# The transpose of one batch's q moved from TensorE to a DMA, in a fused attention and feed-forward kernel

## The chip, the cores and the metric

The kernel runs on one core of one Trainium2 chip. The metric is the device time of one execution in microseconds (us); medians are given with their extremes where a small difference matters. Every run quoted here is of the fast state, the undisturbed one. Ratios are computed as the mean time of one kernel's fast runs over the mean of the other kernel's fast runs in the same rounds, so they are not quite the ratio of the medians quoted beside them.

## The reference

Attention with keys and values averaged over groups of eight positions, then a feed-forward layer with the activation h cos(h):

```python
# q, k, v: (8 batches, 8 heads, 576 positions, 64) float32
k_p = k.reshape(B, H, Sp, 8, D).mean(axis=3)          # Sp = 72
v_p = v.reshape(B, H, Sp, 8, D).mean(axis=3)
attn = softmax(q @ k_p.T / sqrt(D))                   # per batch and head
x = (attn @ v_p), heads side by side                  # 4608 tokens x 512
h = x @ w_in                                          # 512 -> 2048
out = (h * cos(h)) @ w_out                            # 2048 -> 512
```

## The kernel before

Scores are computed as k_pooled (stationary) times q transposed, so q of each batch is transposed in bf16 from 128 partitions x 2304 to 18 blocks of 128x128. For batches 2 to 7 a DMA issued from the SP queue does this from SBUF to SBUF. For batches 0 and 1 TensorE does it, into PSUM, from where VectorE and ScalarE copy it:

```python
    def q_transpose(b):                                   # by DMA
        qT_tile(b)
        nc.sync.dma_start_transpose(out=att["qT", b], in_=q_flat(b))

    def q_transpose_mm(b, bank, g0, g1):                  # on TensorE
        ...
        for g in range(g0, g1):
            nc.tensor.matmul(ps[:, g - g0, :], q_flat(b)[:, g * 128:(g + 1) * 128], identity, is_transpose=True)
        return lambda copy: copy(out=att["qT", b][:, g0:g1, :], in_=ps)
```

Behind the loads for batch 0, the next loads go out in this order, all from GpSimd, converted from float32 to bf16 on the way:

```python
    for cg in range(3):
        load_w_in(cg)
    load_even(staged["k", 1], 1, k)
    load_even(staged["q", 1], 1, q, 0, 2)      # first half of q of batch 1
    load_w_in(3)
    load_even(staged["q", 1], 1, q, 2, 4)      # second half
    load_w_out(0)
    load_even(staged["v", 1], 1, v)
    ...
    for cg in range(1, 4):
        load_w_out(cg)
```

The tile loop has an up phase (x times w_in, eight groups `fp` of eight matmuls) and a down phase (times w_out). Batch b = t + 1 has its attention interleaved in the down phase of tile t. Only for t = 0 are pooled k and transposed q made on TensorE, between the up groups:

```python
            up_mm(t, fp, 2 if fp < 2 else 0)
            between = ()
            if t == 0:
                if fp == 4:
                    puts = pool_k_mm(1, obanks[0], 0, 2), pool_k_mm(1, obanks[1], 2, 4)
                elif fp in (5, 6):
                    g0 = 9 * (fp - 5)
                    puts = q_transpose_mm(1, obanks[0], g0, g0 + 5), q_transpose_mm(1, obanks[1], g0 + 5, g0 + 9)
                if fp in (4, 5, 6):
                    puts[0](vec)
                    between = ((puts[1], act),)
            up_g(t, fp, between)
        ...
        if t == 0:    # (after so many down matmuls, do this)
            fill[1:] = [(2, S_(0, 0)), (8, lambda: pool_v_mm(1, banks[1])), ..., (18, S_(2, 2)), ...]
        ...
        if 0 < t and b + 1 < B:      # later loads wait until k of this batch has been transposed
            nc.gpsimd.tensor_copy(out=gate, in_=kk[b % 2][0:1, 0, 0:1])
```

`S_(0, 0)` is the first scores unit of batch 1.

The softmax here doesn't subtract the row's maximum and nothing guards it: scores larger than these inputs give would overflow.

Of the kernel before, what the change touches and what calls it, by code (L numbers as in the profile page):

```python
# [19 lines left out]
def kernel(  # L20
# [52 lines left out]
    obanks = [psum.tile([128, 512], FP32, name=f"obank{i}") for i in range(2)]  # L73
# [33 lines left out]
    def load_q(b):  # L107
        q_tile(b)
        load_even(staged["q", b], b, q)
# [6 lines left out]
    def load_w_out(cg):  # L116
        nc.gpsimd.dma_start(
            out=w_out_sb[cg],
            in_=moe_w_out[cg * 512:(cg + 1) * 512, :].rearrange("(f p) m -> p f m", p=128))
# [30 lines left out]
    def pool_k_mm(b, bank, pj0, pj1):  # L150

        kb = staged["k", b]
        ps = bank[:, 0:(pj1 - pj0) * Sp].rearrange("p (j n) -> p j n", n=Sp)
        for pj in range(pj0, pj1):
            for t in range(ROW):
                for rows in half:
                    nc.tensor.matmul(ps[rows, pj - pj0, :], lhsT=kb[rows, pj, t, :], rhs=groups[rows, t, :],  # L157
                                     start=(t == 0), stop=(t == ROW - 1))
        return lambda copy: put_kk(b, ps, pj0, pj1, copy)
# [10 lines left out]
    def k_transpose(b):  # L170
        nc.sync.dma_start_transpose(out=kk[b % 2], in_=kp2[b % 2].rearrange("p h s d -> p (h s d)"))
# [4 lines left out]
    def qT_tile(b):  # L176
        att["qT", b] = asb.tile([128, QB, 128], BF16, name="qT", tag="qT")

    def q_flat(b):
        return staged["q", b].rearrange("p j t d -> p (j t d)")  # L180

    def q_transpose(b):
        qT_tile(b)
        nc.sync.dma_start_transpose(out=att["qT", b], in_=q_flat(b))

    def q_transpose_mm(b, bank, g0, g1):

        if ("qT", b) not in att:
            qT_tile(b)
        ps = bank.bitcast(BF16)[:, 0:(g1 - g0) * 128].rearrange("p (g n) -> p g n", n=128)  # L190
# [3 lines that stand above are left out]
# [6 lines left out]
    def scores(b, u, pair):  # L200
        scores_mm(b, u, pair)
        scores_exp(b, u, pair)
# [32 lines left out]
    def values(b, u, pair, later=None):  # L235

        (c0, n), (h0, nh) = u
        ex = att.pop(("ex", b, u))
        for i in range(nh):
            pj, hp = divmod(h0 + i, 2)  # L240
            nc.tensor.matmul(pair[:, hp, (i // 2) * n:(i // 2 + 1) * n],  # L241
                             lhsT=vz[b % 2][:, pj, 2 * hp:2 * hp + 2, :].rearrange("p a d -> p (a d)"),
                             rhs=ex[:, ex_col(u, i):ex_col(u, i) + n])
        w = nh * n // 2
        lnc, inv = inverse_tile(w)
        for hp in range(2):
            nc.scalar.activation(out=lnc[half[1 - hp]], in_=pair[half[1 - hp], hp, 0:w], func=ACTF.Ln)  # L247
        nc.scalar.activation(out=inv, in_=lnc, func=ACTF.Exp, scale=-1.0)  # L248

        def mul():  # L250
            for hp in range(2):
                nc.vector.tensor_mul(out=x_out(b, u, half[hp]), in0=cols(pair[half[hp], hp, :], u),  # L252
                                     in1=cols(inv[half[1 - hp]], u))

        if later is None:
            mul()
        else:
            later.append(mul)
# [25 lines left out]
    def exp_tables():  # L284
        nc.scalar.preload_act_table_set("natural_log_exp_and_others")  # L285

    def sin_tables():
        nc.scalar.preload_act_table_set("trig_and_small")  # L288


    def up_mm(t, fp, k0=0, k1=KCH):

        h = banks[fp % 3]
        for j in range(2):
            fc = 2 * fp + j
            for ki in range(k0, k1):
                nc.tensor.matmul(h[:, j, :], lhsT=w_in_sb[fc // 4][:, ki, (fc % 4) * 128:(fc % 4 + 1) * 128],  # L297
                                 rhs=xT[:, ki, t * TILE:(t + 1) * TILE],
                                 start=(ki == 0), stop=(ki == KCH - 1))

    def up_g(t, fp, between=()):
        h = banks[fp % 3]
        cos = msb.tile([128, 2, TILE], FP32, name="cos", tag="cos", bufs=2)
        nc.scalar.activation(out=cos, in_=h, func=ACTF.Sin, bias=half_pi[:, :1])  # L304
        for put, copy in between:
            put(copy)
        nc.vector.tensor_mul(out=g_sb[:, 2 * fp:2 * fp + 2, :], in0=h, in1=cos)  # L307
# [78 lines left out]
    for cg in range(1, 4):  # L386
        load_w_out(cg)

    def warm_up(n, bank):

        for i in range(n):
            nc.tensor.matmul(bank, lhsT=warm[:, 0:128], rhs=warm)
# [7 lines left out]
    puts = q_transpose_mm(0, banks[2][:, 0, :], 0, 5), q_transpose_mm(0, obanks[0], 5, 9)  # L400
# [24 lines left out]
    for t in range(NT):  # L425
        b = t + 1
        if t > 0:

            up_mm(t, 0, 0, 2)
            up_mm(t, 1, 0, 2)  # L430
        for fp in range(FFCH // 2):
            up_mm(t, fp, 2 if fp < 2 else 0)
            between = ()
            if t == 0:
                if fp == 4:
                    puts = pool_k_mm(1, obanks[0], 0, 2), pool_k_mm(1, obanks[1], 2, 4)
                elif fp in (5, 6):
                    g0 = 9 * (fp - 5)
                    puts = q_transpose_mm(1, obanks[0], g0, g0 + 5), q_transpose_mm(1, obanks[1], g0 + 5, g0 + 9)
                if fp in (4, 5, 6):  # L440
                    puts[0](vec)
                    between = ((puts[1], act),)
            up_g(t, fp, between)
            if 0 < t and b < B:
                if fp == 0:
                    q_transpose(b)
                elif fp == 2:
                    k_transpose(b)
        mms = [(ms, fc) for ms in range(4) for fc in range(FFCH)]
        if t == 0:  # L450
            mms = [(ms, fc) for hm in range(2) for cg in range(4) for ms in range(2 * hm, 2 * hm + 2)
                   for fc in range(4 * cg, 4 * cg + 4)]


        def S_(n, bank):
            return lambda: scores(b, us[n], banks[bank])

        later = []

        def V_(n, bank, wait=None):  # L460
            return lambda: values(b, us[n], banks[bank], wait)

        fill = []
        if t < B:
            exp_tables()
            fill = [(1, lambda: scores(t, REST, banks[2])), (16, lambda: values(t, REST, banks[1]))]
        if t == 0:
            fill[1:] = [(2, S_(0, 0)), (8, lambda: pool_v_mm(1, banks[1])), (8, lambda: values(t, REST, banks[2])),
                        (11, S_(1, 0)), (13, V_(0, 1)), (18, S_(2, 2)), (21, V_(1, 0, later)), (26, S_(3, 1)),
                        (32, lambda: later.pop()()), (32, V_(2, 2)), (40, V_(3, 0))]  # L470
        elif b < B:
            us = BY_TOKENS

            def scores_of(*parts):

                def go():
                    for f in scores_mm, scores_exp:
                        for b_, u, bank in parts:
                            f(b_, u, banks[bank])
                return go  # L480

            fill = [(4, scores_of((b, us[0], 2), (b, us[1], 0))), (14, V_(0, 1, later)), (16, lambda: later.pop()()),
                    (19, V_(1, 2)), (35, scores_of((b, us[2], 0), (b, us[3], 1), (t, REST, 2))),
                    (38, V_(2, 0)), (43, lambda: values(t, REST, banks[1])), (46, V_(3, 2))]
        fi = 0
        if t == NT - 1:
            mms = mms[:-FFCH]
        for n, (ms, fc) in enumerate(mms):
            while fi < len(fill) and fill[fi][0] <= n:
                fill[fi][1]()  # L490
                fi += 1
            down_mm(obanks[ms % 2], ms, fc)
            if fc == FFCH - 1:
                down_out(t, ms, obanks[ms % 2])
        if t < B:
            sin_tables()
        if 0 < t and b + 1 < B:

            nc.gpsimd.tensor_copy(out=gate, in_=kk[b % 2][0:1, 0, 0:1])  # L499
        if b + 1 < B:  # L500
            load_kv(b + 1, "k", k)
            load_q(b + 1)
            load_kv(b + 1, "v", v)
            pool_add(b + 1, "k")
            pool_add(b + 1, "v")
# [29 lines left out]
```

## Time and profile before

| | before |
|---|---|
| median (lowest, highest) | 302.22 us (302.09 to 302.62) |
| span of the profiled execution | 301.4 us |
| TensorE busy | 97% |
| DMA engines busy, 8 to 48 us | 1.2 on the scale where 1 is one packet in flight per engine |
| transposed q of batch 1 first read at | 35.51 us |

The profile lists per engine when instructions ran and what ended the idleness ahead of them. L192 is the line of the TensorE transposes, L297 the up matmuls, L310 the down matmuls, L211 the scores. PEld is TensorE's weight load, which overlaps its matmuls; SPq and POOLq are queues from which DMAs are issued; q0 is the DMA queue of the loads that GpSimd issues, q1 that of what SP issues. The profiled execution of the kernel before took 303.21 us, 1.0 us more than the median.

### The profile page before, as it was taken

The numbers are of one execution on the slowest core, as the hardware profiler recorded it, in microseconds if no ns is written. First come the engines' busy times: TensorE is split into PE (matmuls) and PEld (weight loads), VectorE is DVE, ScalarE is ACT, GpSimd is POOL, SyncE is SP. The second block draws the span as 40 slices with busy tenths as digits, with TensorE's granted clock in tenths as the row PEclk, the third lists the DMA queues.
The fourth block names the chain that finished last, engine by engine and source line by source line (L and its number), as shares of the span: only waits on it lengthen the run. The fifth ranks groups of instructions, "written<-read, shape, count | busy, mean of one in ns | idle before, by whom it ended". The sixth has DMA issues, their size and how long they took to land.

```text
span 301.4 us, 4625 instructions
## 1 busy us (share of the span) xinstructions
PE 293.9 (97%) x1816; PEld 143.2 (48%) x1816; DVE 170.8 (57%) x212; ACT 205.7 (68%) x254; POOL 130.4 (43%) x93
## 2 busy tenths in 40 slices
PE   8789999999999999999999999999999999999995
PEld 3445544445544454445444544455444544444444
DVE  5448637465467446754666556654775477425712
ACT  3786798469876987688778886789668966605500
POOL 8463016984983398239913990389300000000000
PEclk9999999999999999999999999999999999999999
DMA  7999999639526961697079617791811130131023
GB/s 152 197 207 206 206 205 195 141 55 176 117 60 124 167 127 29 146 158 140 6 170 143 129 36 171 94 174 39 141 32 35 37 70 0 37 70 35 0 67 75
DMA packets 44165, 32.91 MB, mean 109 GB/s; under 512 B 22128, under 2 KB 39408, under 8 KB 44144
## 3 DMA queue, kind: packets, MB, share of 16 engines
q0 software_dynamic: 19744, 18.07, 38.3%
q1 hardware_dynamic: 24160, 14.42, 20.5%
q8 instruction: 14, 0.23, 0.3%
q10 hardware_dynamic: 240, 0.13, 0.2%
q14 instruction: 7, 0.06, 0.1%
HBM read 36.70 MB, written 9.44 MB: 153 GB/s over the span
## 4 chain that ended last, share of the span: by engine, by line
PE 93%; DMA 4%; POOL 1%; DVE 1%; issue 0%; POOLq 0%; DVEq 0%
PE bank L297 41%; PE obank L310 41%; PE bank L241 5%; DMA kv_st<-in_v_dram 4%; PE bank L211 3%; PE bank L328 1%; PE bank L165 1%; POOL q_b L84 1%; PE obank L157 0%; PE obank L280 0%; PE obank L192 0%; DVE xT L282 0%; DVE vz L167 0%; POOL kv_st L84 0%; DVE o_sb L316 0%
## 5 line engine op out<-in xcount | busy, mean ns | idle before, releaser
L310 PE MATMUL obank<-w_out_sb,g_sb 128*128 128x512 bf16 x560 | 131.4, 379 | 0.0
L297 PE MATMUL bank<-xT,w_in_sb 128*128 128x512 bf16 x576 | 126.6, 379 | 0.0
L304 ACT ACTIVATE cos<-bank,half_pi 128x1024 f32<-128x1024 f32 x72 | 79.3, 1113 | 59.5 <-PE bank L297 59.5
L307 DVE TENSOR_TENSOR g_sb<-bank,cos 128x1024 bf16<-128x1024 f32 x72 | 87.3, 1223 | 43.0 <-ACT cos L304 42.9
L297 PEld LDWEIGHTS <-w_in_sb 128*128 128x128 bf16 x576 | 56.1, 98 | 67.6 <-issue 1.6
L310 PEld LDWEIGHTS <-g_sb 128*128 128x128 bf16 x560 | 52.8, 98 | 56.5 <-issue 2.0
L252 DVE TENSOR_TENSOR xT<-bank,inv 64x512 bf16<-64x512 f32 (+1 forms) x72 | 45.3, 629 | 40.8 <-ACT inv L248 40.1
L141 POOL TENSOR_TENSOR kv_st<-kv_st 72x2048 f32<-72x2048 bf16 x12 | 48.7, 4058 | 33.9 <-DMA kv_st<-in_k_dram 33.9
L247 ACT ACTIVATE lnc<-bank 64x512 f32<-64x512 f32 (+1 forms) x72 | 39.2, 544 | 3.1 <-PE bank L241 1.7
L316 DVE COPY o_sb<-obank 128x512 f32<-128x512 f32 x35 | 23.6, 689 | 30.9 <-PE obank L310 30.5
L218 ACT ACTIVATE ex<-bank 72x1024 bf16<-72x1024 f32 (+1 forms) x40 | 35.0, 929 | 8.5 <-PE bank L211 8.4
L142 POOL TENSOR_TENSOR kv_st<-kv_st 72x1024 f32<-72x1024 f32 x12 | 28.2, 2349 | 1.0
L248 ACT ACTIVATE inv<-lnc 128x512 f32<-128x512 f32 (+1 forms) x36 | 21.0, 583 | 1.1
L241 PE MATMUL bank<-ex,vz 72*128 72x256 bf16 (+1 forms) x176 | 20.0, 243 | 0.0
L241 PEld LDWEIGHTS <-vz 72*128 72x128 bf16 x176 | 13.6, 97 | 9.6 <-DVE xT L252 0.5
L145 POOL TENSOR_TENSOR kp<-kv_st 72x512 bf16<-72x512 f32 x12 | 14.9, 1263 | 0.5
L211 PE MATMUL bank<-qT,kk 64*72 64x256 bf16 (+1 forms) x192 | 13.2, 252 | 0.0
L211 PEld LDWEIGHTS <-kk 64*72 64x72 bf16 x192 | 7.4, 109 | 9.9 <-issue 7.2
L285 ACT ACT_TABLE_LOAD x9 | 11.5, 1283 | 0.9 <-PEq L519 0.7
L499 POOL COPY gate<-kk 1x1 bf16<-1x1 bf16 x5 | 0.9, 179 | 25.7 <-DMA kk<-kp 25.7
L288 ACT ACT_TABLE_LOAD x9 | 11.5, 1283 | 0.2
L103 POOL DMA_DIRECT2D kv_st<-in_v_dram x6 | 5.0, 841 | 8.8 <-PE bank L165 8.8
(55 smaller groups left out, 93.1 us busy)
## 6 DMA issues: line engine op xcount, KB each, us to landing
out_dram<-o_sb SPq DMA_DIRECT2D x70, 128.0 KB, 2.4
kv_st<-in_v_dram POOLq DMA_DIRECT2D x8, 576.0 KB, 13.7
kv_st<-in_k_dram POOLq DMA_DIRECT2D x7, 576.0 KB, 7.6
q_b<-in_q_dram POOLq DMA_DIRECT2D x6, 576.0 KB, 9.9
w_in_sb<-in_moe_w_in_dram POOLq DMA_DIRECT2D x4, 512.0 KB, 14.5
w_out_sb<-in_moe_w_out_dram POOLq DMA_DIRECT2D x4, 512.0 KB, 18.1
q_b<-in_q_dram POOLq DMA_DIRECT2D x4, 288.0 KB, 13.0
g_sb<-in_k_dram SPq DMA_DIRECT2D x1, 576.0 KB, 3.7
```

The lines of the kernel that those rows point to most:

```text
L141: add(out=s, in0=x[:, :, 0:4, :], in1=x[:, :, 4:8, :], op=ADD)
L142: add(out=s[:, :, 0:2, :], in0=s[:, :, 0:2, :], in1=s[:, :, 2:4, :], op=ADD)
L211: nc.tensor.matmul(pair[:Sp, bank, c:c + n].rearrange("p (g n) -> p g n", n=64), lhsT=kk[b % 2][half[r], h0 + i, 0:Sp], rhs=att["qT", b][h ...
L218: nc.scalar.activation(out=ex[:, 0:nh * n].rearrange("p (a n) -> p a n", a=2), in_=pair[:Sp, :, 0:nh * n // 2], func=ACTF.Exp, scale=scale ...
L241: nc.tensor.matmul(pair[:, hp, (i // 2) * n:(i // 2 + 1) * n], lhsT=vz[b % 2][:, pj, 2 * hp:2 * hp + 2, :].rearrange("p a d -> p (a d)"), ...
L247: nc.scalar.activation(out=lnc[half[1 - hp]], in_=pair[half[1 - hp], hp, 0:w], func=ACTF.Ln)
L252: nc.vector.tensor_mul(out=x_out(b, u, half[hp]), in0=cols(pair[half[hp], hp, :], u), in1=cols(inv[half[1 - hp]], u))
L297: nc.tensor.matmul(h[:, j, :], lhsT=w_in_sb[fc // 4][:, ki, (fc % 4) * 128:(fc % 4 + 1) * 128], rhs=xT[:, ki, t * TILE:(t + 1) * TILE], st ...
L304: nc.scalar.activation(out=cos, in_=h, func=ACTF.Sin, bias=half_pi[:, :1])
L307: nc.vector.tensor_mul(out=g_sb[:, 2 * fp:2 * fp + 2, :], in0=h, in1=cos)
L310: nc.tensor.matmul(o, lhsT=g_sb[:, fc, ms * 128:(ms + 1) * 128], rhs=w_out_sb[fc // 4][:, fc % 4, :], start=(fc == 0), stop=(fc == FFCH - 1))
L316: nc.vector.tensor_copy(out=o[:, 0:n], in_=ps)
```

## The change

The intent is to take 18 transposes and their four copies off the engines at a place where TensorE is the bound, and to let an idle DMA queue do them, as it already does for the later batches.

```diff
     for cg in range(1, 4):
         load_w_out(cg)
 
+    q_transpose(1)
+
     def warm_up(n, bank):
 ...
                 if fp == 4:
                     puts = pool_k_mm(1, obanks[0], 0, 2), pool_k_mm(1, obanks[1], 2, 4)
-                elif fp in (5, 6):
-                    g0 = 9 * (fp - 5)
-                    puts = q_transpose_mm(1, obanks[0], g0, g0 + 5), q_transpose_mm(1, obanks[1], g0 + 5, g0 + 9)
-                if fp in (4, 5, 6):
                     puts[0](vec)
                     between = ((puts[1], act),)
```

## The prediction

> **What bounds the kernel now.** I read the busy table and the chain that ended last on the page, then the timeline of 28 to 47 us, where the change acts, and then the loads by landing time.
>
> ```profile
> PE 293.9 (97%) x1816; PEld 143.2 (48%) x1816; DVE 170.8 (57%) x212; ACT 205.7 (68%) x254; POOL 130.4 (43%) x93
> ...
> PE 93%; DMA 4%; POOL 1%; DVE 1%; issue 0%; POOLq 0%; DVEq 0%
> ```
>
> TensorE is busy 97% of the span and is 93% of the chain. Its instructions run in program order, so an instruction taken off it is worth its time, and an instruction that waits moves the whole rest of the kernel back by that wait. The timeline (start, length, engine) around the two places where q of batch 1 is now transposed:
>
> ```profile
> 28.43 1.90 PE L297 MATMUL bank<-xT,w_in_sb 128*128 128x512 bf16 x8
> ...
> 30.16 0.67 PE L192 MATMUL obank<-identity,q_b 128*128 128x128 bf16 x9
> ...
> 30.66 1.89 PE L297 MATMUL bank<-xT,w_in_sb 128*128 128x512 bf16 x8
> ...
> 32.39 0.67 PE L192 MATMUL obank<-identity,q_b 128*128 128x128 bf16 x9
> ...
> 32.89 1.89 PE L297 MATMUL bank<-xT,w_in_sb 128*128 128x512 bf16 x8
> ...
> 34.62 0.38 PE L310 MATMUL obank<-w_out_sb,g_sb 128*128 128x512 bf16 x1
> ...
> 35.51 0.41 PE L211 MATMUL bank<-qT,kk 64*72 64x256 bf16 x4
> ```
>
> A group of eight up matmuls with nine transposes takes 30.66 - 28.43 = 2.23 us, a group without them 34.62 - 32.89 = 1.73 us. The last line is the first reader of the transposed q of batch 1: it follows only two down matmuls and the last scores of batch 0, 35.51 us into the span. That is the **deadline**.
>
> Meanwhile the DMA engines are full. In the table of two-microsecond stretches (the last two columns are DMA share and GB/s), every row from 8 us to 48 us looks like these two, and they fall off only after 50 us:
>
> ```profile
> 30.00:32.00 2.00, 2.00 (x18) 1.18 (x17) 1.45 (x3) 1.59 (x2) 0.00 (x0) 1.00 1.23 207
> 34.00:36.00 2.00, 2.00 (x19) 0.84 (x18) 0.99 (x2) 1.34 (x3) 0.00 (x0) 1.00 1.23 205
> ```
>
> So the loads are a backlog, one after another. The second half of q of batch 1 is issued at 11.41 us (operation on its tile, window 11 to 12 us) and lands 18.9 us later, at **30.3 us**:
>
> ```profile
> L84 POOL DMA_DIRECT2D q_b<-in_q_dram x1: 696/696/696, 11.4 to 11.4; - x1
> ...
> DMA to landing us min/median/max: 18.9/18.9/18.9
> ```
>
> By the same reckoning (issue plus time to landing) w_out 0 lands at 32.9, v of batch 1 at 35.7, w_out 1 at 38.2, w_out 2 at 40.7, w_out 3 at 43.3, k of batch 2 at 47.7, q of batch 2 at 50.0 us. Only v of batch 2 is not yet issued (38.7 us, after the pooling of v of batch 1 has freed its buffer).
>
> **What the Trainium skill says.** (1) VectorE: DVE Perf Modes, section The three transpose paths, gives 390 ns for a 128x128 bf16 transpose on TensorE and 1309 ns by DMA. The trace is better for both: nine on TensorE cost 0.50 us of its time (56 ns each), and a DMA of 18 blocks lands in 4.2 us, 0.23 us a block. (2) Advanced Engine Details and Errata, section X-Bar Transpose (TRN2), says that transposing DMAs are as fast as ordinary ones, and speaks of 16-row wavefronts. The trace agrees on the rate in a free moment (1133 packets, 290 GB/s between 59 and 60 us). (3) DMA: Bandwidth & Descriptors, section Queues, rings and completion order, says that each DMA engine goes round-robin between its queues and switches only between whole packets. The trace agrees that a sharing queue is slowed: see below. (4) TensorE: Matmul & The Clock Gate, Part 1, says that TensorE falls to half rate after some 3.4 us of idleness and needs as long of work to get back. The trace shows the cold state at its start: ten 128x512 matmuls take 4.45 us, 0.445 us each, against 1.73 / 8 = 0.216 us later.
>
> **The change part by part.**
> Removed: 18 transposes on TensorE in two groups of nine, 2 x (2.23 - 1.73) = **1.0 us** off the path; also two copies of 0.49 us on VectorE and two of 0.58 us on ScalarE, which lie beside up matmuls that are the longer (1.73 us against 1.23 + 0.49 and 1.11 + 0.58) and are worth nothing.
> Added: one DMA transpose of 128x2304 bf16 on the SP queue, which has nothing else to do before its first output at 46.05 us. It can start when the second half of q has landed: 30.3 us, plus about 0.25 us from a landing to the start of what it releases (w_in 3 lands at 28.9, the issue that waits for it starts at 29.17), so 30.55 us. The deadline is 35.51 - 1.0 = 34.5 us. That leaves 4.0 us. The six such transposes of later batches need 4.2 us from issue to landing (4.1 to 5.6) with the load queue empty. So even undisturbed it would be just late, by about half a microsecond, counting 0.25 us again for the reader.
>
> But here it isn't undisturbed. No transpose in this trace runs beside loads: the kernel holds the loads of later batches back until a transpose has landed (the one-element copy "gate"). So I size it from two other things.
> First, output writes, which share the SP queue. On the page 70 of them have a median of 2.4 us; those issued between 45.9 and 47.2 us, beside the loads, took 5.1 us, though each has only 64 packets, four per DMA engine:
>
> ```profile
> out_dram<-o_sb SPq DMA_DIRECT2D x70, 128.0 KB, 2.4
> ```
>
> ```profile
> q0 software_dynamic: 249, 0.27, 123.3%
> out_dram<-o_sb SPq DMA_DIRECT2D x2, 128.0 KB, 5.1
> ```
>
> That is 2.7 us more for four packets: 0.7 us a turn on the slowest engine (estimate).
> Second, the last transpose (214.8 us, 5.6 us to landing). In tenths of a microsecond its traffic runs at some 110 packets, then a single instruction fetch (16 KB: 0.23 MB in 14) occupies one engine, and all sixteen stop for 0.5 us and crawl until 219.4 us. A transpose moves at the pace of its slowest engine.
> The transpose has some 2304 packets of 256 bytes, 144 per engine, and takes 2.0 us of pure transfer (2304 / 1133 a us); the other 2.2 us of 4.2 are fixed. If it changes turns after 16 rows (the wavefront; my choice, no trace shows it), it has nine turns: 9 x 0.7 = 6.3 us of waiting if each turn is a slow one, 9 x 0.3 = 2.7 us if they are average ones (in 48.0 to 49.0 us 48 output packets passed on 16 engines, one per 0.33 us). So landing takes 4.2 + 2.7 = 6.9 to 4.2 + 6.3 = 10.5 us. I take **10 us**, near the slow end because of the lockstep.
> The first scores then start at 30.55 + 10 + 0.25 = 40.8 us in place of 35.51: **+5.3 us**, with the 1.0 us saved already in it. TensorE stands idle some 40.8 - 34.5 = 6.3 us, more than the 3.4 us, so it will run the next 3.4 us or so of work at half rate: about **+1.7 us**. Sum: +7.0 us, 302.2 + 7.0 = 309.2, say 309.
> Moved: the transpose takes 2 us of all DMA engines from the loads, so w_out 1 to 3 land 2 us later (40.2, 42.7, 45.3). Their first uses come at 38.6 us (w_out 1) and later before; delayed by 5 us they no longer wait. Later stages should just shift: k and q of batch 2 have 6 us to spare (the transposed k lands at 62.5 us, read at 68.8).
>
> **The rivals.**
> A: *the transfer is hidden*. It needs landing within 4 us, which not even the free ones did. And without the wait for q, w_out 1 takes its place: it landed at 38.2 for a use at 38.6 us; 1.0 us earlier and with the load 2 us later, TensorE would wait for it until 40.4. So the gain of 1.0 us cannot be had, and the least I expect is +1.5 us, 303.7. A real gain of 2% is out of reach: only 1.0 us is removed.
> B: *mild sharing*: landing in 6 to 8 us, scores 1.3 to 3.3 us late, little or no cold clock: 303.7 to 306.
> C: *starved*: the transpose gives way after each 256-byte packet. 144 turns of 0.3 us are 43 us, longer than the backlog, so it would land only when the loads have run dry at 50 + 2 us: +17 us and 2 us of cold clock, 321. For it: outputs beside loads land 5 us after issue in each batch. Against it: those outputs got through before the backlog ended.
> D: VectorE or ScalarE becoming the bound: no, both only lose work.
>
> **Range and chances.** The 2% line is +6.0 us, at a landing time of about 9.4 us. B and the upper half of my main case lie under it, the rest and C over it. I give slower 0.6, within 2% 0.38, faster 0.02. Range 304 to 321, from just over the floor of rival A to rival C.
>
> **What would show it.** In the trace after: no transposes in the two up groups, 1.73 us each; a DMA transpose issued on SP at about 30.5 us with 7 to 12 us to landing; the first scores of batch 1 waiting for it on TensorE, until about 41 us; the matmuls after it at twice their time for some 3 us if the idleness was over 3.4 us; from 60 us on the same stages as before, all shifted by one amount. I am wrong if the transpose lands within 6 us beside the loads, if it starts at another time than 30.5 us because it waits for some other transfer, or if the clock stays warm.

## The result, and the profile after

The kernel after takes 319.76 us (319.27 to 320.99), the kernel before 302.15 us in the same rounds: a ratio of 1.0586 (95% interval 1.0553 to 1.0619), **5.9% slower**, 17.6 us.

The busy table, the TensorE clock in 40 slices and the chain that ended last, from the page of the kernel after:

```profile
PE 291.4 (92%) x1766; PEld 141.9 (45%) x1798; DVE 169.9 (54%) x210; ACT 204.8 (65%) x252; POOL 130.6 (41%) x93
...
PEclk9999756999999999999999999999999999999998
...
PE 81%; DMA 15%; ACT 1%; issue 1%; POOL 1%; DVE 0%; POOLq 0%; SPq 0%
```

TensorE fell from 97% to 92% busy, and DMA rose from 4% to 15% of the chain. The clock row shows a dip in slices 5 to 7, which are 32 to 56 us. The timeline of TensorE there (start, length, engine, line; in brackets how long the engine had been idle and what ended it):

```profile
33.49 0.39 PE L310 MATMUL obank<-w_out_sb,g_sb 128*128 128x512 bf16 x1
49.88 0.64 PE L211 MATMUL bank<-qT,kk 64*72 64x256 bf16 x4 [16.00 <-DMA qT<-q_b]
50.45 2.63 PE L310 MATMUL obank<-w_out_sb,g_sb 128*128 128x512 bf16 x6
53.02 1.17 PE L165 MATMUL bank<-kv_st,groups 64*72 64x256 bf16 x18
```

The same stretch before:

```profile
35.19 0.39 PE L310 MATMUL obank<-w_out_sb,g_sb 128*128 128x512 bf16 x1
35.51 0.41 PE L211 MATMUL bank<-qT,kk 64*72 64x256 bf16 x4
35.85 1.47 PE L310 MATMUL obank<-w_out_sb,g_sb 128*128 128x512 bf16 x6
37.25 1.17 PE L165 MATMUL bank<-kv_st,groups 64*72 64x256 bf16 x18
```

After, there is one wait of 16.0 us, for the transpose. Behind it six down matmuls take 2.63 us, which took 1.47 us before, and then the pace is as before. The DMA issues of the window 30 to 31 us (size or count, then time from issue to landing), and SP's own timeline:

```profile
qT<-q_b SPq DMA_TRANSPOSE x1, 19.4
```

```profile
30.40 9.35 SPq L184 DMA_TRANSPOSE qT<-q_b  x1
```

The transpose was issued when it was expected, at 30.4 us, but took 19.4 us to land, against 4.1 to 5.6 us for the six of the later batches. The DMA queues between 36 and 38 us (packets, MB, share of 16 engines), before and then after, show beside what it ran:

```profile
q0 software_dynamic: 415, 0.41, 124.4%
```

```profile
q0 software_dynamic: 312, 0.31, 91.2%
q1 hardware_dynamic: 314, 0.08, 30.1%
```

Before, the load queue alone moved 415 packets in those two microseconds. After, both queues moved the same number, 312 and 314. A load packet is about 1 KB (0.31 MB over 312), a transpose packet 256 bytes. So the transpose moves at 157 packets a us, not the 1133 it reaches alone: 2304 / 157 = 14.7 us. Its first packets appear at 34.3 us, and 34.3 + 14.7 = 49.0 us; the landing at 49.8 us fits. That it fits so closely is in part luck, as the rate was not constant: 192 and 225 packets a us from 42 to 44 us, where the load packets were shorter (0.14 and 0.12 MB), and 106 to 163 from 44 to 49 us. In that last stretch the load queue fell from 92% to 41% of the engines' time, and the transpose did not speed up for it.

The sum in the trace: the scores start 16.1 us later after the second down matmul than before (49.88 - 33.49 against 35.51 - 35.19), the slow clock adds 1.4 us between the scores and the pooling of v (3.14 us against 1.74), the removed transposes bring TensorE to this place 1.0 us earlier: +16.5 us. The two profiled executions themselves differ by 319.27 - 303.21 = 16.1 us, of which -0.7 is the earlier start of the up phase. The medians differ by 1.5 us more than those two, as the profiled run of before was slow by 1.0 and that of after fast by 0.5.

### The profile page after: what moved, and what is told of

It is laid out like the page before. It is cut to its first block, busy times and chain, and to the rows that moved or that the text cites. A ratio compares the mean times of both kernels' runs of the same rounds, so it can differ in the third digit from the quotient of the medians.

```text
span 317.5 us, 4555 instructions
## 1 busy us (share of the span) xinstructions
PE 291.4 (92%) x1766; PEld 141.9 (45%) x1798; DVE 169.9 (54%) x210; ACT 204.8 (65%) x252; POOL 130.6 (41%) x93
## 3 DMA queue, kind: packets, MB, share of 16 engines
q1 hardware_dynamic: 26496, 15.01, 20.7%
## 4 chain that ended last, share of the span: by engine, by line
PE 81%; DMA 15%; ACT 1%; issue 1%; POOL 1%; DVE 0%; POOLq 0%; SPq 0%
PE obank L310 38%; PE bank L297 34%; DMA q_b<-in_q_dram 9%; DMA qT<-q_b 6%; PE bank L241 5%; PE bank L211 3%; PE bank L328 1%; ACT ex L218 1%; DVE g_sb L307 0%; ACT cos L304 0%; PE bank L165 0%; POOL q_b L84 0%; POOL kv_st L84 0%; DVE o_sb L316 0%; POOL row_of L347 0%
## 5 line engine op out<-in xcount | busy, mean ns | idle before, releaser
L316 DVE COPY o_sb<-obank 128x512 f32<-128x512 f32 x35 | 23.7, 690 | 30.9 <-PE obank L310 30.5
L211 PE MATMUL bank<-qT,kk 64*72 64x256 bf16 (+1 forms) x192 | 13.4, 254 | 16.2 <-DMA qT<-q_b 16.0
L84 POOL DMA_DIRECT2D q_b<-in_q_dram x10 | 7.8, 781 | 24.0 <-DMA qT<-q_b 23.2
L167 DVE CAST vz<-bank 72x512 bf16<-72x512 f32 x2 | 1.4, 687 | 21.4 <-PE bank L165 18.8
## 6 DMA issues: line engine op xcount, KB each, us to landing
w_out_sb<-in_moe_w_out_dram POOLq DMA_DIRECT2D x4, 512.0 KB, 20.1
```

What stands on the lines that cost most here:

```text
L211: nc.tensor.matmul(pair[:Sp, bank, c:c + n].rearrange("p (g n) -> p g n", n=64), lhsT=kk[b % 2][half[r], h0 + i, 0:Sp], rhs=att["qT", b][h ...
L316: nc.vector.tensor_copy(out=o[:, 0:n], in_=ps)
```

## The experiments

**Theory (turns):** beside the loads the transpose passes one 256-byte packet for each load packet, so 2304 packets need about 15 us; TensorE waits for this, and then runs on a cold clock. **Rivals:** (R1) this transpose is slow in itself (first of its kind, or SP, which the issue held 9.35 us, generates it slowly); (R2) the loads that it delays are what costs the time; (R3) it lands only once the backlog of loads has run dry; (R4) the queues share by bytes or time, not by packets. All kernels below gave a result within the reference's tolerance.

### The removal alone

```diff
# kernel after, with
-    q_transpose(1)
+    att["qT", 1] = att["qT", 0]     # just ahead of the tile loop; wrong on purpose
```

> Wrong result on purpose: the TensorE transposes of q of batch 1 are gone and nothing takes their place (the scores of batch 1 read the transposed q of batch 0). If removing them is worth its whole 1.0 us: about 301.2 us. If, as the prediction's rival A says, the load of w_out 1 (landing at 38.2 us for a use at 38.6) becomes the wait: about 302.0 us, with TensorE waiting on that load in the down phase of the first tile.

Measured: 302.45 us (301.62 to 302.73) against 302.28 us, ratio 1.000 (0.998 to 1.002). (The result still passed the comparison, though batch 1 is computed from batch 0's q: with these inputs the comparison is not sharp enough to see it.) TensorE's timeline has a wait that was not there before:

```profile
37.55 0.81 PE L310 MATMUL obank<-w_out_sb,g_sb 128*128 128x512 bf16 x3 [0.64 <-DMA w_out_sb<-in_moe_w_out_dram]
```

What follows: removing the transposes is worth nothing measurable, even if the transposed q came for free. The gain of 1.0 us runs into the load of w_out 1, as the prediction's rival A had it; 0.64 us of the 1.0 us is visible in this line, and the rest is within the scatter of the times. With the loads as they are, the change had nothing to win.

### The addition alone

```diff
# kernel before, with
     for cg in range(1, 4):
         load_w_out(cg)
+    spare = wpool.tile([128, QB, 128], BF16, name="spare")
+    nc.sync.dma_start_transpose(out=spare, in_=q_flat(1))   # nobody reads it
```

> The kernel before, with the DMA transpose added into a spare buffer that nobody reads: the cost of the sharing to the loads alone. If transpose and loads take turns packet for packet (156 packets a us each, loads slowed by a fifth), the transpose takes about 19 us here too, w_out 1 to 3 land 1 to 3 us later and TensorE waits 1 to 3 us for them: 303 to 305 us. If the 17.6 us were the loads' delay and not the wait for the transpose, it would be near 319 us.

Measured: 306.10 us against 302.28 us, ratio 1.0130 (1.0115 to 1.0145), so +3.8 us. The transpose takes as long as in the kernel after (operation on the spare buffer), and TensorE waits for w_out three times (who waited for whom: total, times, longest):

```profile
DMA to landing us min/median/max: 20.7/20.7/20.7
```

```profile
PE obank L310 <- DMA w_out_sb<-in_moe_w_out_dram: 3.0, 3, 1.4
```

What follows: R2 is a real cost, but of 3.8 us and not of 17.6. It can be estimated from this trace. The queues share from 33.8 us on, and w_out 3, the last load that TensorE waits for, lands at 46.3 us (42.8 us in the run of the removal alone). The load queue passes a quarter fewer packets while it shares (312 in place of 415): about 2.9 us of loading lost. On top of it both queues stop for some 0.9 us. Behind an instruction fetch of 16 KB (queue q8, 38.0 to 38.2 us) they pass only 57 and 56 packets from 39 to 40 us, in place of some 155 each. The runs that kept TensorE busy and that moved only the second half (below) have such a stop too (21 and 24 packets from 40 to 41 us; 49 and 39 from 41 to 42 us), each behind a fetch while the transpose was under way. In the kernel before, a fetch in 38 to 39 us leaves the loads at 205 and 199 packets a us, and in the kernel after none falls into the transfer. So a fetch during the transpose goes with the stop in all three profiles that have one; no run tests it alone. In the kernel after the loads' delay is hidden: no wait for w_out shows, because TensorE is standing still for the transpose anyway. The expected 303 to 305 us was somewhat too low.

### TensorE kept busy during the wait

```diff
# kernel after, with
-            fill[1:] = [(2, S_(0, 0)), ...
+            fill[1:] = [(2, lambda: warm_up(72, banks[0][:, 0, :])), (2, S_(0, 0)), ...
```

> The kernel after, with 72 dummy matmuls (15.6 us at full rate) on TensorE just ahead of the first scores of batch 1, where it stands idle for 16.0 us. If the half rate after the idleness costs the 1.5 us that the trace shows (2.96 us of work at half rate): about 318.3 us and six down matmuls in 1.3 us, not 2.63. If the clock is no part of it: 319.8 us.

Measured: 318.19 us (317.97 to 319.09), ratio 1.0532 to before, 1.6 us less than the kernel after, though 72 matmuls were added. The end of the dummies and what follows:

```profile
33.60 15.70 PE L394 MATMUL bank<-warm 128*128 128x512 bf16 x72
50.26 0.41 PE L211 MATMUL bank<-qT,kk 64*72 64x256 bf16 x4 [0.96 <-DMA qT<-q_b]
50.60 1.47 PE L310 MATMUL obank<-w_out_sb,g_sb 128*128 128x512 bf16 x6
```

The six down matmuls are back at 1.47 us and the mean granted clock of the run is 1.00, where the kernel after has 0.97. So 1.6 us of the loss is the cold clock, about what was expected (1.5 us); the other 16 are the wait.

### The transpose alone on the DMA engines

```diff
# kernel after, with
     load_even(staged["q", 1], 1, q, 2, 4)
+    q_transpose(1)
+    nc.gpsimd.tensor_copy(out=gate, in_=att["qT", 1][0:1, 0, 0:1])
     load_w_out(0)
     load_even(staged["v", 1], 1, v)
 ...
-    q_transpose(1)
```

> The kernel after, with every load that is queued behind q of batch 1 held back until the transpose has landed (a one-element copy from its result ahead of them). If the loads beside it are the cause: 4 to 5 us from issue to landing, not 19.4, and SP is held 2.1 us by the issue, not 9.35; the time is then set by the late w_out loads, some 307 to 309 us. If this first transpose is slow for another reason (its place in the kernel, the descriptor generation on SP): still about 19 us to landing and well over 320 us.

Measured: the transpose lands 4.0 us after its issue, and SP is held 2.14 us. This is the DMA issues view of 28 to 31 us:

```profile
qT<-q_b SPq DMA_TRANSPOSE x1, 4.0
```

The same instruction, issued at 29.7 us (30.4 us in the kernel after), with no loads beside it: R1 falls. Nor did SP's long issue set the rate in the kernel after: it ended at 39.75 us, and the transpose passed 160 packets from 39 to 40 us and 156 from 40 to 41 us. Its first packet appears 1.25 us after the issue (30.9 us), against 3.9 us in the kernel after. The time is 311.43 us (ratio 1.0307), longer than the 307 to 309 us expected, because TensorE now waits 6.7 us for w_out 0, which could not be issued before 34.0 us, and then also runs cold:

```profile
39.57 0.59 PE L310 MATMUL obank<-w_out_sb,g_sb 128*128 128x512 bf16 x1 [6.73 <-DMA w_out_sb<-in_moe_w_out_dram]
```

### Only the later loads held back

```diff
# kernel after, with
     load_even(staged["v", 1], 1, v)
 ...
+    q_transpose(1)
+    nc.gpsimd.tensor_copy(out=gate, in_=att["qT", 1][0:1, 0, 0:1])
     for cg in range(1, 4):
         load_w_out(cg)
-    q_transpose(1)
```

> The kernel after, with only w_out 1 to 3 and the loads after them held back until the transpose has landed; w_out 0 and v of batch 1 stay beside it (some 5 us of loads). Turn theory: the transpose shares for those 5 us and then runs alone, 6 to 8 us to landing, not 19.4 and not 4.0; TensorE then waits for w_out 1 (landing near 42 us) instead: 306 to 309 us. If holding back loads were free, it would come near 302.

Measured: 7.7 us from issue to landing, as expected, and 309.74 us (308.92 to 311.37; ratio 1.0257), just above the 306 to 309 us expected. TensorE waits 4.0 us for the transpose and runs cold once more; it then waits 0.9 us at the 17th down matmul, which is for w_out 2 and not, as expected, for w_out 1. Between no loads beside it (4.0 us), some 4 us of loads (7.7 us) and loads throughout (19.4 us) the landing follows the loads.

### More backlog behind it

In the kernel after GpSimd issued the load of q of batch 2 only at 50.4 us, 23.2 us after it was free to, because it waited for the transpose. That came from writing the transpose high up in the program: q of batch 2 was then given the buffer of batch 1's q and not of batch 0's (I infer this; what is shown is the wait, and that it goes with the place).

```diff
# kernel after, with
     for cg in range(1, 4):
         load_w_out(cg)
-    q_transpose(1)
 ...
     sin_tables()
+    q_transpose(1)
     for t in range(NT):
```

> The kernel after, with the same transpose written further down in the program (before the first tile's loop), so that q of batch 2 should get the other buffer and its load no longer wait 23 us for the transpose. If turns are taken packet for packet, more backlog changes nothing: 20 to 21 us to landing, 319 to 321 us. If the backlog's length set the landing: some 3 us later, 323 us.

Measured: the load of q of batch 2 goes out at 28.6 us again, so 2.5 us more of loads stand beside the transpose; it takes 20.1 us to land, and the time is 320.0 us (319.61 to 320.24), as in the kernel after within the scatter. R3 falls: the landing isn't set by the length of the backlog.

### Load packets half as long

```diff
# kernel after, with load_w_out as two DMAs
+        for m0 in (0, 256):
             nc.gpsimd.dma_start(
-                out=w_out_sb[cg], in_=moe_w_out[cg * 512:(cg + 1) * 512, :]...)
+                out=w_out_sb[cg][:, :, m0:m0 + 256], in_=moe_w_out[cg * 512:(cg + 1) * 512, m0:m0 + 256]...)
```

> The kernel after, with each w_out load in two halves of 256 columns, so that its packets are half as long (512 bytes written) and twice as many. If a transpose packet waits for one load packet whatever its length: equal packet counts of both queues in each stretch, both well over 156 a us beside w_out loads, and the transpose lands sooner, 13 to 17 us from issue. If the engines share by bytes or time: as slow as before, 19 to 21 us. The total time may still be bad because the w_out loads get slower.

Measured: 14.7 us from issue to landing, and 314.57 us (ratio 1.0413), 5.2 us faster than the kernel after. The same stretch of 36 to 38 us as above:

```profile
q0 software_dynamic: 485, 0.24, 87.3%
q1 hardware_dynamic: 489, 0.13, 47.3%
```

Again equal counts, and both 1.56 times those of the kernel after (489 against 314). The transpose's packets are unchanged; only the loads' packets got shorter, and the transpose got faster by it. That excludes R4: a share by bytes or by time would not come out at equal counts for 1 KB and for 512-byte packets alike. What the counts can't tell is whether the queues alternate packet by packet or in larger groups of equal number.

### The transpose in two halves

```diff
     def q_transpose(b):
         qT_tile(b)
-        nc.sync.dma_start_transpose(out=att["qT", b], in_=q_flat(b))
+        parts = ((0, 9), (9, 18)) if b == 1 else ((0, 18),)
+        for g0, g1 in parts:
+            nc.sync.dma_start_transpose(out=att["qT", b][:, g0:g1, :], in_=q_flat(b)[:, g0 * 128:g1 * 128])
```

> The kernel after, with the transpose cut in two of nine blocks, the first of which can start when the first half of q lands (about 25.6 us), four microseconds sooner. If the transpose's rate is one packet per load packet (156 a us, so 14.8 us for all 2304, after 3.6 us before the first): the second half lands about 4.5 us sooner than in the kernel after, the scores start near 45.5 us, and the time is 315 us. If the landing is set by the end of the load backlog and not by the rate: no sooner, 319.8 us.

Measured: 308.76 us (307.76 to 308.98), ratio 1.0221: 11 us faster than the kernel after, where I expected 4.5. My rate was right: the second half lands 16.2 us after 29.7, at 45.9 us. What I had missed is who reads which half. The first scores read heads 0 to 3, which lie in the first half, and it lands 12.9 us after 25.3, at 38.2 us:

```profile
38.23 0.64 PE L213 MATMUL bank<-qT,kk 64*72 64x256 bf16 x4 [4.58 <-DMA qT<-q_b]
```

TensorE is let go there, and the second half is in time for its own reader at 46.05 us. The run changes two things at once, which it doesn't separate: the first half starts 4.4 us earlier than the second (25.3 against 29.7 us), and its reader no longer waits for the other half. An estimate for the second: in the kernel after 1152 packets, half of all, had passed by 41.9 us (the sum of its counts per us), 8 us before the landing; if packets pass in the order of the blocks, which no run shows, that much of the 16 us was waiting for data that the next instruction did not need.

### Half on each

The obvious mixture: the half that is needed first stays on TensorE, the half needed later goes to the DMA.

```diff
# kernel before, with
+    qT_tile(1)
+    nc.sync.dma_start_transpose(out=att["qT", 1][:, 9:18, :], in_=q_flat(1)[:, 9 * 128:18 * 128])
 ...
-                elif fp in (5, 6):
+                elif fp == 5:
 ...
-                if fp in (4, 5, 6):
+                if fp in (4, 5):
```

> The kernel before, with nine of the 18 blocks still transposed on TensorE (the half that the first scores read) and only the second nine by DMA: half the removal, half the packets, and a reader that comes later (the third unit of scores, near 40.5 us). By the turn rate of 156 packets a us: first packet 3.7 us after the issue at 29.7, 1152 packets in 7.4 us, landing about 41.8 us, so a wait of some 1.3 us; w_out 1 and 2 are late by half of what they were in the run that only added the transpose, about 1 us of waits; 0.5 us saved on TensorE: 303.5 to 305 us, so worse than before by less than 1%. If the removal were worth its 0.5 us and the second half were hidden: 301.7 us.

Measured: 305.36 us (304.71 to 306.68), ratio 1.0117 (1.0086 to 1.0148): still slower than before, and just above the 303.5 to 305 us expected. The expected wait of 1.3 us for the transpose did not come: it lands 13.1 us after 29.6 us, at 42.7 us, and its reader, held up by w_out itself, starts at 43.29 us. What is left is the loads' delay:

```profile
PE obank L310 <- DMA w_out_sb<-in_moe_w_out_dram: 2.6, 2, 1.5
```

I had expected about 1 us of these waits. Some 0.9 us of the 2.6 is probably the stop behind an instruction fetch described above, which here falls right before the second wait. Even with that taken off, a fully hidden transpose of half of q costs more (some 1.7 us of waits) than the 0.5 us that it takes off TensorE. No version found here beats the kernel before, and the run of the removal alone says why: right behind TensorE's transposes stand the loads, and with the transposes gone it waits for w_out 1 instead.

| kernel | median us | ratio to before | issue to landing, us |
|---|---|---|---|
| after | 319.76 | 1.0586 | 19.4 |
| removal alone | 302.45 | 1.0000 | none |
| addition alone | 306.10 | 1.0130 | 20.7 |
| kept busy | 318.19 | 1.0532 | 20.5 |
| alone on the DMA engines | 311.43 | 1.0307 | 4.0 |
| later loads held back | 309.74 | 1.0257 | 7.7 |
| more backlog | 320.00 | 1.0589 | 20.1 |
| short load packets | 314.57 | 1.0413 | 14.7 |
| two halves | 308.76 | 1.0221 | 12.9 and 16.2 |
| second half only | 305.36 | 1.0117 | 13.1 |

## Why the prediction was right or wrong

The direction, the path and the place were right; the size was not. It said 309.0 us, +7 us, and +17.6 us came.

- **Removal worth 1.0 us on TensorE, and not to be had:** right on both. Three up groups without transposes take 5.19 us in the kernel after (27.73 to 32.92), 1.73 us each; and the run of the removal alone gains nothing.
- **Issue at 30.55 us:** right, 30.40 us.
- **Landing after 10 us: this is the step that failed.** It was put together as 2.2 us fixed, 2.0 us of transfer and about 6 us of waiting in "nine turns" of 16 rows at 0.3 to 0.7 us each. The term for the waiting was mis-sized: as many load packets pass as transpose packets, 2304 of each, so that the transfer and its waiting take 14.7 us in place of about 8. The fixed part was short too: with the loads beside it the first packet came 3.9 us after the issue, without them 1.25, so 2.6 us more; why it comes so late is not shown. 10 + 6.7 + 2.6 = 19.3 us, and 19.4 were measured. I had chosen the group of 16 without a trace behind it, and had taken the price of a turn from output writes, which have only four packets per engine; their added 2.7 us is close to that late start, and so probably says more of the start than of the turns (not tested).
- **The rivals:** C named the right unit, the single 256-byte packet, but with a wrong price, 0.3 us a turn (it is 16 engines / 157 packets a us = 0.10 us), and a wrong end, the backlog running dry. Its 321 us comes near the result by the two errors balancing; the run with more backlog shows that the backlog's end was not what mattered. A's description of w_out 1 held, but its floor of +1.5 us was too low: even the unread transpose cost 3.8 us, because it takes a quarter of the loads' rate for as long as it shares (about 2.9 us until w_out 3 has landed) and not only the 2.0 us of its own transfer; in that run the stop of some 0.9 us came on top.
- **The 2% line:** a slip. By the prediction's own sums +6.0 us belongs to a landing time of 9.0 us and not 9.4 (30.55 + 9.0 + 0.25 - 35.51 + 1.7 = 6.0); nothing rests on it.
- **Half rate after the idleness, +1.7 us:** right, 1.6 us by the run that was kept busy.
- **Later stages only shift:** right. Between the end of that wait and the end of the kernel no new wait for a DMA shows on TensorE; span minus start of the scores is 301.4 - 35.5 = 265.9 us before and 317.5 - 49.9 = 267.6 us after, the difference being the cold clock.
- **Missed:** that the first scores need only half of q (two halves: 308.76 us), and that the new place in the program would move the load of the next q (which cost nothing).

## What to carry to other kernels

Price a DMA that will run beside a backlog of others by counting packets: here a transfer of many small packets passed as many as the queue beside it, so the time of its transfer was about its packet count times the time in which one packet of each passed (2304 times 1/157 us), and its own free-running time (4 us) said nothing. Before taking work off the busiest engine, ask which wait stands right behind it: an experiment that removes the work and puts nothing in its place shows at once what there is to win, and here it was nothing. If such a transfer must stay, cut it along what its readers need and start each piece when its source lands.

## What the Trainium skill lacked or had wrong

- Advanced Engine Details and Errata, section X-Bar Transpose (TRN2), says that transposing DMAs are as fast as regular ones. That roughly holds alone (4.0 us for 0.59 MB, against 3.4 us for the ordinary load of that size which SP issues at the start); beside loads the same DMA took 19.4 to 20.7 us, and the page has no word on sharing.
- DMA: Bandwidth & Descriptors, section Queues, rings and completion order, has the round-robin between queues with packets of some 9 to 17 descriptors. What a reader needs for an estimate is missing: two busy queues passed equal numbers of the profile's packets (312 and 314; 485 and 489), whatever their lengths, so beside 1 KB packets the queue with the 256-byte packets moved a quarter of the other's bytes (0.08 against 0.31 MB).
- No page that I read gives the later start: first packet 1.25 us after the issue on idle DMA engines, 3.9 us behind a backlog.
- No page that I read has the stop of all DMA traffic behind an instruction fetch during a transpose (57 and 56 packets in a us in place of some 155 each, in the run of the addition alone).
- TensorE: Matmul & The Clock Gate, Part 1, has the clock fall after an idle window of about 3.4 us that runs free. The runs agree that the lag varies: the granted clock fell 1.9 us after the last matmul in the kernel after, 3.0 us with the later loads held back, and more than 3.8 us in the run with two halves. The 1.9 us is shorter than a whole window as the page has it.
